# Attention scores as row-tiled products over one pool of PSUM banks, with keys kept on chip by head

## The chip, the cores and the metric

The kernel runs on one core of a Trainium2 chip. The metric is the device time of one execution in microseconds. Inputs and outputs are in DRAM; the host only lays the arrays out (transposed and padded copies) before the launch.

The engines are TensorE (PE in the profile, with its weight loads as PEld), VectorE (DVE), ScalarE (ACT), GpSimd (POOL) and SyncE (SP, which only issues transfers here). TensorE writes its products into PSUM, eight banks of 128 partitions by 512 floats.

## The reference, cut to what matters

```python
x = A_x                                            # [1, 2048, 448]
g = sigmoid((x * gate_w).sum(-1, keepdims=True))
# a: attention, 16 heads of 28
q, k, v = split_heads(x @ wqkv)
p = softmax(einsum("bhqd,bhkd->bhqk", q, k) * 28 ** -0.5)
a = merge_heads(einsum("bhqk,bhkd->bhqd", p, v)) @ wo
# b: layer norm and MLP, 448 -> 1792 -> 448
h = gelu(einsum("bsd,df->bsf", layernorm(x), w1) + b1)
b = einsum("bsf,fd->bsd", h, w2) + b2
return g * a + (1 - g) * b
```

All of it is float32. The kernel's fast matrix products take a rounded form of float32 (`F32R`, rows marked fp32r). Where more precision is needed an operand is split into a rounded part "hi" and the rest "lo", and hi x hi, hi x lo and lo x hi are added up (in the scores before also lo x lo).

## The kernel before, in words

The work has three stages, one after the other on TensorE, whose order is that of the text (`manual_schedule` for PE at the launch). The other engines' order is chosen by the framework's scheduler.

*Projections (L123 to L243).* The 2048 tokens are four chunks of 512 (`NC`, `CH`). For each chunk seven products of 128 columns give q and k for all heads, written to DRAM as hi and lo (`qk`, L164), and four products give v, padded to 32 columns a head with a column of ones (`vs`). Layer-norm statistics run beside them.

*MLP (L355 to L422).* For each chunk and each of 14 blocks of the hidden layer, `mlp1` accumulates 11 products into one bank (`ph`), ScalarE computes GELU twice (rounded and full), POOL takes the difference, and `mlp2` adds 12 products into four banks (`acc2`). The sum goes to DRAM (`gbs`).

*Attention (L503 to L567).* Heads are taken four at a time (`NG` = 4 groups), queries 512 at a time: 16 chunks (g, c). For each of 16 blocks of 128 keys (k), a step does this:

- `scores` (L522), twice for two heads each: one product a head. Its stationary operand has 113 rows: k hi, lo, hi, lo stacked, 28 rows each, and a row of ones; its moving operand has q hi, lo, lo, hi stacked in the same way and a row with the negative maximum of each query's scores. So one product gives all four hi/lo terms less the maximum. The two heads go to a pair of banks (`psc`, two pairs in turn).
- one exponential on ScalarE for each pair, 128 x 1024 (L531).
- `pv_mm` (L534) for the step before: four products of 32 columns, one for each head, side by side in one bank (`ppv`), in full float32 (two weight halves each, so eight rows in the profile).
- `filler.run` (L314): row maxima, below.

At a chunk's end `finish` (L459) copies the values' bank (L464), sends the four rows of sums through DRAM so that their reciprocals (L467) come back spread over all partitions (L465, L469, L471), normalises on POOL (L475 to L477), and in four later steps projects with `wo` (`project`, L449), adding into `acc` (L455). `STEPS` says in which steps k these pieces come. `finish_last` does the same for the last chunk without the trip through DRAM.

*Row maxima.* `row_max` (L245) finds the maximum of the scores from the hi parts alone: for each chunk 64 products of 28 rows (a head's 128 queries against 512 keys, L280), each in the row group of its head (`32 * j`), each with a `reduce_max` on VectorE (L282), then a transpose and a write to DRAM (`ms`); 65 turns a chunk, 1040 in all. `Filler` spreads these turns evenly over the products of the MLP (400 of them, `MLP_MAX`) and the steps of attention (the other 640), three at a time. Their banks are three of their own (`mp3` in the MLP, `paux` in attention; `paux` also serves `project`). Their keys and queries (`kd`, `qd`) are loaded separately.

*Loads for attention.* `load_k` fills `kring`, twelve buffers that were the MLP's w1 tiles, with one head's half of the keys, hi and lo, twice over; `load_q` fills `qring`. The first group's come late in the MLP (L411 to L416); values (`load_v`), `wo` and the MLP's sums (`acc`, L515, with bias and gate on POOL at L517 and L518) come at the start of attention.

Of the kernel before, what the change touches and what calls it, by code (L numbers as in the profile page):

```python
# [15 lines left out]
P = 128  # L16
S = 2048
# [13 lines left out]
MLP_MAX = 400  # L31
# [7 lines left out]
def kernel(ctx: ExitStack, tc: tile.TileContext, xt, wqk, wv, wo, xk, w1, b1, w2, b2,  # L39
# [22 lines left out]
    ones = dram.tile([8, P], F32, name="ones")  # L62
    rls = dram.tile([NG * NC, 4, CH], F32, name="rls")

    one_t = const.tile([8, P], F32, name="one_t")
# [6 lines left out]
    aq = ctx.enter_context(tc.tile_pool(name="aq", bufs=1, side="right"))  # L72

# [6 lines left out]
    kring = []  # L80
    qring = [aq.tile([P, 4, CH], F32R, name=f"qst{i}") for i in range(3)]

    def load_w(f, pool1, pool, stage):
        r1 = stage.tile([P, 4, P], F32, name="r1")
        nc.sync.dma_start(r1, w1[f])
        t = pool1.tile([P, 8, P], F32R, name=f"w1f{f}")
        w1h[f], w1l[f] = t[:, 0:4], t[:, 4:8]
        if f >= 2:
            kring.append(t.rearrange("p a b -> p (a b)"))
# [11 lines left out]
    def ln_load(c, t):  # L101
# [4 lines left out]
        lnx[c, t] = my.tile([P, CH], F32, name="xr", bufs=4)  # L106
        nc.sync.dma_start(lnx[c, t], xt[t, :, cs])

    def ln_apply(c, t):
        if t == 0:  # L110
            yh[c] = qring[c % 2]
            yl[c] = my.tile([P, 3, CH], F32R, name="yl")
# [10 lines left out]
    with tc.tile_pool(name="qx", bufs=2) as qx, tc.tile_pool(name="qo", bufs=3) as qo, \  # L123
            tc.tile_pool(name="qw", bufs=1) as qw, tc.tile_pool(name="qp", bufs=8, space=PSUM) as qp:
        wh, wl = {}, {}

# [26 lines left out]
        def qk_tile(c, m):  # L153
            ps = qp.tile([P, CH], F32, name="ps")
# [12 lines left out]
        def v_tile(tt):  # L167
            c, i = divmod(tt, TPC)
            sl = slice(i * P, (i + 1) * P)
            ps = qp.tile([P, CH], F32, name="ps")  # L170
# [28 lines left out]
        def ln_turn():  # L199
            ps = qp.tile([P, CH], F32, name="ps")  # L200
# [44 lines left out]
    def row_max(pool):  # L245

        kds, qds = {}, {}

        def load(n):
            g, c = divmod(n, NC)  # L250
            if c == 0:
                kds[g] = mpool.tile([P, S], F32R, name="kd")
                for j in range(4):
                    r = D + (4 * g + j) * DH
                    pool[1].dma_start(kds[g][32 * j:32 * j + DH].bitcast(F32), qk[0, r:r + DH])
            qds[n] = mpool.tile([P, CH], F32R, name="qd")
            for j in range(4):
                r = (4 * g + j) * DH
                pool[1].dma_start(qds[n][32 * j:32 * j + DH].bitcast(F32), qk[0, r:r + DH, c * CH:(c + 1) * CH])

        def close(n, mf):
            g, c = divmod(n, NC)
            ps = pool[0]()
# [3 lines left out]
            pool[1].dma_start(ms[g][:, c * CH:(c + 1) * CH].rearrange("j (i x) -> j i x", x=P), mt.bitcast(F32))  # L267
# [3 lines left out]
        for n in range(NG * NC):  # L271
            kd, qd = kds[n // NC], qds[n]
            mx = mpool.tile([P, 4, TPC, 4], F32, name="mx")
            done = 0
            for i in range(TPC):
                for k in range(4):
                    for j in range(4):
                        ps = pool[0]()
# [16 lines left out]
    class Filler:  # L295


        def __init__(self):
            self.pool = [None, None]
            self.it = row_max(self.pool)  # L300
# [3 lines left out]
        def spread(self, pool, queue, upto, slots):  # L304
            self.pool[:] = pool, queue
            self.first, self.upto, self.slots, self.slot = self.done, upto, slots, 0

        def run(self, n=1, group=1):
# [4 lines left out]
            group = min(group, self.upto - self.done)  # L313
            if due >= group:  # L314
                for _ in range(group):
                    next(self.it, None)
                    self.done += 1
# [3 lines left out]
    HS = S // 2  # L321
    NK = 12
    kst, qst = {}, {}
    nk = nq = 0

    def load_k(g, j, h):

        nonlocal nk
        t = kring[nk % NK]
        if nk < NK:  # L330
            nc.sync.dma_start(t[4 * DH:4 * DH + 1].bitcast(F32),
                              ones.rearrange("a b -> (a b)").rearrange("(o t) -> o t", o=1))
        nk += 1
        kst[g, j, h] = t
        r0 = D + (4 * g + j) * DH
        src = qk[:, r0:r0 + DH, h * HS:(h + 1) * HS]
        for r in range(0, 4 * DH, 2 * DH):
            nc.sync.dma_start(t[r:r + 2 * DH].bitcast(F32), src)

    def load_q(g, c):  # L340

        nonlocal nq
        t = qring[(0, 2, 1)[nq % 3]]
        nq += 1
        qst[g, c] = t
        cs = slice(c * CH, (c + 1) * CH)
        for i, n in enumerate((0, 1, 1, 0)):
            nc.sync.dma_start(t[i * DH:(i + 1) * DH].bitcast(F32),
                              qk[n, 4 * g * DH:4 * (g + 1) * DH, cs].rearrange("(j p) t -> p j t", p=DH))
        nc.sync.dma_start(t[4 * DH:4 * DH + 1].bitcast(F32), ms[g][:, cs].rearrange("(o j) t -> o j t", o=1))  # L350


    ak = ctx.enter_context(tc.tile_pool(name="ak", bufs=1, reuse_waits="tile"))
    with tc.tile_pool(name="mw", bufs=1, reuse_waits="tile") as mw, \
            tc.tile_pool(name="mh", bufs=3, reuse_waits="tile") as mh, \  # L355
            tc.tile_pool(name="mp1", bufs=1, space=PSUM, reuse_waits="tile") as mp1, \
            tc.tile_pool(name="mp3", bufs=3, space=PSUM, reuse_waits="tile") as mp3, \
            tc.tile_pool(name="mp2", bufs=4, space=PSUM, reuse_waits="tile") as mp2:
        hh, hl = {}, {}

        def mlp1(c, f):
            ps = mp1.tile([P, CH], F32, name="ph")
# [4 lines left out]
            for i, (a, b) in enumerate(ops):  # L367
                nc.tensor.matmul(ps, a, b, start=(i == 0), stop=(i == len(ops) - 1))  # L368
                filler.run(1, MG)
# [7 lines left out]
        acc2 = {}  # L377

        def mlp2(c, f):
            for i in range(TPC):  # L380
                if f == 0:
                    acc2[c, i] = mp2.tile([P, D], F32, name="acc2")
                sl = slice(i * P, (i + 1) * P)
                a = acc2[c, i]
                nc.tensor.matmul(a, hh[c, f][:, sl], w2h[f], start=(f == 0), stop=False)  # L385
                nc.tensor.matmul(a, hh[c, f][:, sl], w2l[f], start=False, stop=False)  # L386
                filler.run(2, MG)
                nc.tensor.matmul(a, hl[c, f][:, sl], w2h[f], start=False, stop=(f == NF - 1))  # L388
                filler.run(1, MG)
                if f == NF - 1:  # L390
# [6 lines left out]
                    (nc.sync if c < NC - 1 else nc.gpsimd).dma_start(gbs[tt], gb)  # L397

        prev = None
        for s in range(NC * NF):  # L400
            c, f = divmod(s, NF)
            if c == 0 and f + 2 < NF:
                load_w(f + 2, ak, mw, my)
            if s == FS:
                filler.spread(lambda: mp3.tile([P, 512], F32, name="pm"), nc.sync, MLP_MAX, (NC * NF - FS) * 23)
# [4 lines left out]
            if c == NC - 1 and f == 10:  # L410
                for j in range(4):  # L411
                    load_k(0, j, 0)
                load_q(0, 0)
                for j in range(4):
                    load_k(0, j, 1)
# [8 lines left out]
    def sb(name, bufs):  # L424
        return ctx.enter_context(tc.tile_pool(name=name, bufs=bufs, reuse_waits="tile"))

    av = sb("av", 2)
# [3 lines left out]
    psc = ctx.enter_context(tc.tile_pool(name="psc", bufs=2, space=PSUM, reuse_waits="tile"))  # L431
    ppv = ctx.enter_context(tc.tile_pool(name="ppv", bufs=1, space=PSUM, reuse_waits="tile"))
    paux = ctx.enter_context(tc.tile_pool(name="paux", bufs=3, space=PSUM, reuse_waits="tile"))

    vg = {}

    def load_v(g):
        vg[g] = av.tile([P, NT, P], F32, name="vg")
        for t in (slice(0, 4), slice(4, NT)):
            nc.scalar.dma_start(vg[g][:, t], vs[t, :, g, :].rearrange("t p d -> p t d"))  # L440

    def aux():
        return paux.tile([P, 512], F32, name="aux")

    woh = aw.tile([P, NG, D], F32R, name="woh")
    wol = aw.tile([P, NG, D], F32R, name="wol")
    acc = aw.tile([P, NT, D], F32, name="acc")

    def project(g, tt, oh, ol):  # L449

        po = aux()[:, :D]
# [32 lines left out]
    def finish_last(g, c, pv):  # L484
# [5 lines left out]
        psl = psc.tile([P, 2, CH], F32, name="sc")[:, 0]  # L490
# [12 lines left out]
    load_v(0)  # L503
    for g in range(NG):
        worw = ao.tile([P, D], F32, name="ob")
        nc.gpsimd.dma_start(worw, wo[:, g])
        nc.vector.tensor_copy(woh[:, g], worw)
        nc.gpsimd.tensor_sub(wol[:, g], worw, woh[:, g].bitcast(F32))

# [4 lines left out]
    for c in range(NC):  # L514
        nc.gpsimd.dma_start(acc[:, c * TPC:(c + 1) * TPC], gbs[c * TPC:(c + 1) * TPC].rearrange("t p d -> p t d"))  # L515
        for tt in range(c * TPC, (c + 1) * TPC):
            nc.gpsimd.tensor_add(acc[:, tt], acc[:, tt], b2b)  # L517
            nc.gpsimd.tensor_scalar(acc[:, tt], acc[:, tt], ngate[:, tt:tt + 1], None, op0=OP.mult)  # L518

    filler.spread(aux, nc.gpsimd, NG * NC * 65, (NG * NC - 2) * NT + LQ - 1)  # L520

    def scores(g, c, k, jj):  # L522

        h, kk = divmod(k, NT // 2)
        ps = psc.tile([P, 2, CH], F32, name="sc")
        for i in range(2):
            j = 2 * jj + i
            nc.tensor.matmul(ps[:, i], kst[g, j, h][:4 * DH + 1, kk * P:(kk + 1) * P],  # L528
                             qst[g, c][:4 * DH + 1, j], start=True, stop=True)
        t = ap.tile([P, 2, CH], F32, name="pt")  # L530
        nc.scalar.activation(t, ps, AF.Exp, scale=SCALE)  # L531
        return t

    def pv_mm(g, c, k, pv, pt):  # L534
        for j in range(4):
            nc.tensor.matmul(pv[32 * j:32 * j + 32, :], vg[g][:, k, 32 * j:32 * j + 32], pt[j // 2][:, j % 2],  # L536
                             start=(k == 0), stop=(k == NT - 1), skip_group_check=True)

    fin = None
    todo = []  # L540
    for g in range(NG):
        for c in range(NC):
# [78 lines left out]
```

## Time and profile before

| what | value |
|---|---|
| median of three runs | 1275.13 us (1271.72 to 1276.21) |
| profiled execution, its own time | 1273.18 us |
| its span in the profile | 1271.2 us |
| mean granted TensorE clock | 0.962 of full speed |
| instructions in the span | 16167 |
| bytes moved by DMA | 101.44 MB |
| MLP's last product on TensorE starts | 502.70 us |
| attention's last values products end | 1256.86 us |

The span runs from the first to the last instruction of the program; the time has 2.0 us around it. In the rows that follow, a group of instructions has its line, engine, operation, what it writes and reads with the shapes, its count, busy time, the mean length of one, and the idle time of its engine just before it with what ended that. A row of the timeline has start, length, engine, line and the number of instructions merged into it. A window's row gives the busy time of each engine in that stretch. Products overlap on TensorE, so a busy TensorE need not be at its peak.

### The profile page before, as it was taken

The numbers are of one execution on the slowest core, as the hardware profiler recorded it, in microseconds if no ns is written. First come the engines' busy times: TensorE is split into PE (matmuls) and PEld (weight loads), VectorE is DVE, ScalarE is ACT, GpSimd is POOL, SyncE is SP. The second block draws the span as 40 slices with busy tenths as digits, with TensorE's granted clock in tenths as the row PEclk, the third lists the DMA queues.
The fourth block names the chain that finished last, engine by engine and source line by source line (L and its number), as shares of the span: only waits on it lengthen the run. The fifth ranks groups of instructions, "written<-read, shape, count | busy, mean of one in ns | idle before, by whom it ended". The sixth has DMA issues, their size and how long they took to land.

```text
span 1271.2 us, 16167 instructions
## 1 busy us (share of the span) xinstructions
PE 1196.9 (94%) x6085; PEld 653.2 (51%) x6085; DVE 775.9 (61%) x1298; ACT 645.0 (51%) x765; POOL 322.5 (25%) x362
## 2 busy tenths in 40 slices
PE   7998999999999998196999999999999999999997
PEld 6886667766677665032444434444434444444433
DVE  3543377877776776144676757666756777676703
ACT  5243522212212211164677757767657767767784
POOL 4022952311222112356222121112022202211220
PEclk9999899999999999588999989999989999999998
DMA  8987740100101212532013142102412111210001
GB/s 281 295 279 261 203 108 25 46 9 1 37 16 47 72 53 82 147 112 59 17 40 75 53 103 78 38 10 56 99 64 61 44 31 38 76 35 34 25 24 58
DMA packets 56053, 101.44 MB, mean 80 GB/s; under 512 B 7352, under 2 KB 24240, under 8 KB 55528
## 3 DMA queue, kind: packets, MB, share of 16 engines
q1 hardware_dynamic: 41640, 82.53, 21.0%
q0 software_dynamic: 6016, 13.70, 4.0%
q10 hardware_dynamic: 8320, 4.19, 1.5%
q8 instruction: 48, 0.79, 0.3%
q14 instruction: 29, 0.24, 0.1%
HBM read 73.76 MB, written 26.49 MB: 79 GB/s over the span
## 4 chain that ended last, share of the span: by engine, by line
PE 75%; DMA 14%; POOL 5%; issue 2%; DVE 2%; ACT 1%; SPq 1%; ACTq 0%; POOLq 0%; DVEq 0%
PE sc L528 20%; PE pv L536 17%; PE ph L368 11%; PE aux L280 7%; PE pm L280 5%; PE acc L388 4%; PE acc L385 4%; PE acc L386 3%; DMA w1f<-qk 3%; DMA lt<-ob 2%; DMA xraw<-in_xt 2%; DMA acc<-gbs 2%; POOL acc L518 1%; PE ps L160 1%; PE aux L454 1%
## 5 line engine op out<-in xcount | busy, mean ns | idle before, releaser
L531 ACT ACTIVATE pt<-sc 128x1024 f32<-128x1024 f32 x512 | 496.5, 1021 | 230.6 <-PE sc L528 219.8
L282 DVE TENSOR_REDUCE mx<-aux 128x1 f32<-128x512 f32 x630 | 396.2, 683 | 176.8 <-PE aux L280 176.3
L528 PE MATMUL sc<-qst,w1f 113*128 113x512 f32 x1024 | 317.5, 429 | 33.9 <-ACT pt L531 33.9
L282 DVE TENSOR_REDUCE mx<-pm 128x1 f32<-128x512 f32 x394 | 248.1, 684 | 92.0 <-PE pm L280 91.6
L536 PE MATMUL pv<-pt,vg 128*32 128x512 f32 x2048 | 279.3, 617 | 0.0
L528 PEld LDWEIGHTS sc<-qst,w1f 113*128 113x128 f32 x1024 | 172.7, 191 | 152.5 <-ACT pt L531 83.6
L373 ACT ACTIVATE hh<-ph,b1s 128x512 fp32r<-128x512 f32 x56 | 38.4, 686 | 247.5 <-PE ph L368 247.5
L368 PE MATMUL ph<-qst,w1f 128*128 128x512 f32 x448 | 152.2, 413 | 7.1 <-ACT h L374 7.0
L280 PEld LDWEIGHTS aux<-kd,qd 28*128 28x128 f32 x630 | 45.0, 184 | 199.6 <-DVE mx L282 123.6
L375 POOL TENSOR_TENSOR hl<-h,hh 128x512 fp32r<-128x512 f32 x56 | 73.1, 1305 | 245.6 <-ACT h L374 244.3
L280 PE MATMUL aux<-kd,qd 28*128 28x512 f32 x630 | 116.7, 503 | 14.5 <-DVE mx L282 14.3
L368 PEld LDWEIGHTS ph<-qst,w1f 128*128 128x128 f32 x448 | 84.3, 192 | 34.3 <-issue 11.0
L536 PEld LDWEIGHTS pv<-pt,vg 128*32 128x32 f32 x2048 | 40.8, 108 | 92.5 <-issue 86.1
L388 PE MATMUL acc<-w2h,hl 128*128 128x448 f32 x224 | 87.2, 389 | 0.0
L385 PE MATMUL acc<-w2h,hh 128*128 128x448 f32 x224 | 84.5, 377 | 0.0
L386 PE MATMUL acc<-w2l,hh 128*128 128x448 f32 x224 | 82.0, 366 | 0.0
L465 POOL DMA_DIRECT2D lt<-ob x15 | 10.7, 716 | 254.3 <-DVE ob L464 254.3
L280 PE MATMUL pm<-kd,qd 28*128 28x512 f32 x394 | 73.5, 497 | 1.2 <-DVE mx L282 0.4
L368 PE MATMUL ph<-yl,w1f 128*128 128x512 f32 x168 | 69.5, 414 | 0.0
L455 DVE SCALAR_TENSOR_TENSOR acc<-aux,gate,acc 128x448 f32<-128x448 f32 x64 | 43.4, 678 | 39.3 <-PE aux L454 39.3
L280 PEld LDWEIGHTS pm<-kd,qd 28*128 28x128 f32 x394 | 28.2, 182 | 48.8 <-DVE mx L282 36.0
L160 PE MATMUL ps<-xh,wh 128*128 128x512 f32 x112 | 45.5, 406 | 7.0 <-ACT xh L147 6.4
(99 smaller groups left out, 980.8 us busy)
## 6 DMA issues: line engine op xcount, KB each, us to landing
qk<-hl SPq DMA_DIRECT2D x28, 512.0 KB
qst<-qk SPq DMA_DIRECT2D x64, 224.0 KB
w1f<-qk SPq DMA_DIRECT2D x64, 224.0 KB
xraw<-in_xt SPq DMA_DIRECT2D x16, 256.0 KB
vs<-vt SPq DMA_DIRECT2D x16, 256.0 KB
xr<-in_xt SPq DMA_DIRECT2D x16, 256.0 KB
rc<-rls POOLq DMA_DIRECT2D x60, 64.0 KB, 2.3
bxr<-in_xk SPq DMA_DIRECT2D x8, 448.0 KB
```

The source lines that it names most:

```text
L160: nc.tensor.matmul(ps, a, b, start=(i == 0), stop=(i == len(ops) - 1))
L280: nc.tensor.matmul(ps, qd[r, i * P:(i + 1) * P], kd[r, k * 512:(k + 1) * 512], start=True, stop=True)
L282: nc.vector.reduce_max(mx[:, j, i, k:k + 1], ps, axis=AX)
L368: nc.tensor.matmul(ps, a, b, start=(i == 0), stop=(i == len(ops) - 1))
L375: nc.gpsimd.tensor_sub(hl[c, f], h, hh[c, f].bitcast(F32))
L385: nc.tensor.matmul(a, hh[c, f][:, sl], w2h[f], start=(f == 0), stop=False)
L386: nc.tensor.matmul(a, hh[c, f][:, sl], w2l[f], start=False, stop=False)
L388: nc.tensor.matmul(a, hl[c, f][:, sl], w2h[f], start=False, stop=(f == NF - 1))
L455: nc.vector.scalar_tensor_tensor(acc[:, tt], po, gate[:, tt:tt + 1], acc[:, tt], op0=OP.mult, op1=OP.add)
L528: nc.tensor.matmul(ps[:, i], kst[g, j, h][:4 * DH + 1, kk * P:(kk + 1) * P], qst[g, c][:4 * DH + 1, j], start=True, stop=True)
L531: nc.scalar.activation(t, ps, AF.Exp, scale=SCALE)
L536: nc.tensor.matmul(pv[32 * j:32 * j + 32, :], vg[g][:, k, 32 * j:32 * j + 32], pt[j // 2][:, j % 2], start=(k == 0), stop=(k == NT - 1), s ...
```

## The change

Scores no longer use a stacked operand. The four heads of a group lie 32 partitions apart, so that each has a row group of TensorE to itself. Each head takes three products (lo x lo is left out), k hi x q hi (with the row of ones and the maximum, 29 rows), k lo x q hi and k hi x q lo (28 rows), added in one bank. The twelve products of a step are issued in an order and into banks that a class `Banks` works out while the program is built: it keeps an estimate, in units of one product, of when each of seven banks is free, and gives scores, row maxima and projections the banks that are free first. The eighth bank holds the values. The program has one PSUM tile of eight banks from start to end.

Keys are loaded once for each group, hi and lo apart (`khi`, `klo`), and `khi` serves the row maxima too, so `kd` goes. `load_khi`, `load_klo`, `load_q`, `load_qm` (the maxima) and `load_v` for the first group stand within the MLP; loads of later groups, `wo` and `acc` stand at given steps of attention, all on SP. Row maxima: 460 turns in the MLP, two or three at a time in attention, none in step k = 0. In attention all engines keep the order of the text. The step's order is now scores, row maxima, values of the step before, pieces of `finish`.

```diff
-MLP_MAX = 400
+MLP_MAX = 460
...
+    khi = [aq.tile([P, S], F32R, name=f"khi{g}") for g in range(2)]
+    qbuf = [(aq.tile([P, CH], F32R, name="qh0"), aq.tile([P, CH], F32R, name="ql0"))]
+    klob, vgb = [aq.tile([P, S], F32R, name="klo0")], [aq.tile([P, NT, P], F32, name="vg0")]
...
+    bank = ctx.enter_context(tc.tile_pool(name="pbank", bufs=1, space=PSUM)).tile([P, 8, CH], F32, name="bank")
...
-        r2 = stage.tile([P, D], F32, name="r2")
+        r2 = stage.tile([P, D], F32, name="r2", bufs=1)
...
-            kd, qd = kds[n // NC], qds[n]
+            kd, qd = khi[n // NC], qds[n]
...
-                        ps = pool[0]()
+                        ps = env.bank(j)
...
+            n = min(most, left, max(least, int(due)))
+            for _ in range(n):
+                next(self.it, None)
+                self.done += 1
+            return n
...
+    def load_khi(g):
+        for j in range(4):
+            r = D + (4 * g + j) * DH
+            nc.sync.dma_start(khi[g][32 * j:32 * j + DH].bitcast(F32), qk[0, r:r + DH])
+        nc.sync.dma_start(khi[g][DH:P:32].bitcast(F32),
+                          ones.rearrange("(a b) x -> a (b x)", a=1).partition_broadcast(4).rearrange("a o x -> a (o x)"))
...
+    def load_q(n):
+        g, c = divmod(n, NC)
+        qs[n] = qbuf[n % 3]
+        for i in range(2):
+            for j in range(4):
+                r = (4 * g + j) * DH
+                nc.sync.dma_start(qs[n][i][32 * j:32 * j + DH].bitcast(F32), qk[i, r:r + DH, c * CH:(c + 1) * CH])
+    def load_qm(n):
+        g, c = divmod(n, NC)
+        nc.sync.dma_start(qs[n][0][DH:P:32].bitcast(F32), ms[g][:, c * CH:(c + 1) * CH])
...
+            if s == FS - 1:
+                load_khi(0)
...
-            if c == NC - 1 and f == 10:
-                for j in range(4):
-                    load_k(0, j, 0)
-                load_q(0, 0)
-                for j in range(4):
-                    load_k(0, j, 1)
+            if c == 1 and f == 8:
+                load_khi(1)
+            if c == 2 and f == 10:
+                load_klo(0)
+                load_q(0)
+                load_qm(0)
+            if c == 3 and f == 1:
+                load_v(0)
...
+    class Banks:
...
+        def tile(self, tiled):
+            if tiled != self.tiled:
+                self.pe = max([self.pe + 0.4] if tiled else [r + 0.9 for r in self.rows])
+                self.rows = [self.pe] * 4
+                self.tiled = tiled
+        def product(self, j, ready):
+            self.pe = max(self.pe, self.rows[j], ready)
+            self.rows[j] = self.pe + 1
+            return self.pe + 1
+        def heads(self):
+            self.tile(True)
+            o = sorted(range(7), key=lambda b: self.free[b])[:4]
+            o = sorted(o[:2]) + sorted(o[2:])
+            ready = [max(self.pe, self.free[b]) for b in o]
+            turns = sorted((ready[j] + i, j, i) for j in range(4) for i in range(3))
+            end = [0.0] * 4
+            for _, j, i in turns:
+                end[j] = self.product(j, ready[j])
+            for i in (0, 2):
+                self.act = max(self.act, max(end[i:i + 2]) + 0.9) + 4.5
+                for b in o[i:i + 2]:
+                    self.free[b] = self.act + 0.5
+            return o, [t[1:] for t in turns]
+        def take(self, j=None):
+            b = min(range(7), key=lambda b: self.free[b])
+            self.tile(j is not None)
+            if j is None:
+                self.pe = end = max(self.pe, self.free[b]) + 2.8
+            else:
+                end = self.product(j, self.free[b])
+            self.dve = max(self.dve, end + 0.9) + 3
+            self.free[b] = self.dve + 0.5
+            return bank[:, b]
+        def values(self):
+            self.tile(False)
+            self.pe = max(self.pe, self.last) + 4.4
+            self.last = self.act + 0.5
...
+    def scores(g, c, k):
+        o, turns = banks.heads()
+        ks = slice(k * P, (k + 1) * P)
+        qh, ql = qs[g * NC + c]
+        for j, i in turns:
+            a, b, n = ((khi[g], qh, DH + 1), (klo[g], qh, DH), (khi[g], ql, DH))[i]
+            r = slice(32 * j, 32 * j + n)
+            nc.tensor.matmul(bank[:, o[j]], a[r, ks], b[r], start=(i == 0), stop=(i == 2))
+        pt = []
+        for i in (0, 2):
+            t = ap.tile([P, 2, CH], F32, name="pt")
+            nc.scalar.activation(t, bank[:, o[i]:o[i + 1] + 1:o[i + 1] - o[i]], AF.Exp, scale=SCALE)
+            pt.append(t)
+        return pt
...
+    with tc.manual_schedule(engines={E.SP, E.Pool, E.Activation, E.DVE}):
...
+                if g == 0:
+                    if k == 6:
+                        load_acc(c)
+                    if k == 14:
+                        gate_acc(c)
+                if k == 1 and n + 1 < NG * NC:
+                    load_q(n + 1)
+                if k == LQ and n + 1 < NG * NC:
+                    load_qm(n + 1)
+                if g + 1 < NG:
+                    if c == 1 and k == 4:
+                        load_klo(g + 1)
+                    if c == 2 and k == 4:
                         load_v(g + 1)
...
+                pt = scores(g, c, k)
+                if k:
+                    filler.run(1, 2, 3)
+                else:
+                    filler.run(1, 99, 0)
+                if todo:
+                    pv_mm(*todo)
+                    if todo[2] == NT - 1:
+                        fin = finish(todo[0], todo[1], todo[3])
+                        next(fin)
+                todo = (g, c, k, pv, pt)
                 if fin is not None and k in STEPS:
                     next(fin, None)
```

More of the change, by code (lines that the diff above doesn't have):

```diff
@@ L153, in qk_tile @@
         def qk_tile(c, m):
-            ps = qp.tile([P, CH], F32, name="ps")
+            ps = next_ps()
             ops = []
@@ L311, in run @@
+        def run(self, n=1, least=1, most=1):
             self.slot += n
             due = self.first + (self.upto - self.first) * min(1, self.slot / self.slots) - self.done
[L313 to L317, printed above, removed]
-    filler = Filler()
[L321 to L353, printed above, removed]
+            left = self.upto - self.done
@@ L447 @@
+    banks = Banks()
     acc = aw.tile([P, NT, D], F32, name="acc")
+    for i in (1, 2):
+        qbuf.append((aw.tile([P, CH], F32R, name=f"qh{i}"), aw.tile([P, CH], F32R, name=f"ql{i}")))
     def project(g, tt, oh, ol):
-        po = aux()[:, :D]
+        po = banks.take()[:, :D]
         nc.tensor.matmul(po, oh, woh[:, g], start=True, stop=False)
@@ L489, in finish_last @@
         ol = ao.tile([P, CH], F32R, name="ol")
-        psl = psc.tile([P, 2, CH], F32, name="sc")[:, 0]
+        psl = banks.take()
         tiles = [slice(i * P, (i + 1) * P) for i in range(TPC)]
@@ L513 @@
     nc.vector.tensor_scalar(ngate, gate, -1.0, 1.0, op0=OP.mult, op1=OP.add)
[L514 to L532, printed above, removed]
+    filler.spread(banks.take, nc.gpsimd, NG * NC * 65, (NG * NC - 2) * NT + LQ - 1)
+    def scores(g, c, k):
[12 more added lines that the diff above has]
+        return pt
     def pv_mm(g, c, k, pv, pt):
```

173 lines of the change are left out of this document (90 added, 83 removed).

## The prediction

> **What bounds the kernel now.** The page's engine rows first, then its chain of waits.
>
> ```profile
> PE 1196.9 (94%) x6085; PEld 653.2 (51%) x6085; DVE 775.9 (61%) x1298; ACT 645.0 (51%) x765; POOL 322.5 (25%) x362
> PE 75%; DMA 14%; POOL 5%; issue 2%; DVE 2%; ACT 1%; SPq 1%; ACTq 0%; POOLq 0%; DVEq 0%
> L280 PEld LDWEIGHTS aux<-kd,qd 28*128 28x128 f32 x630 | 45.0, 184 | 199.6 <-DVE mx L282 123.6
> ```
>
> TensorE is busy 94% of the span and holds 75% of the chain, but that is an average over three stages. So next the windows, one for each stage: first the projections, then the MLP, the change-over into attention, and attention.
>
> ```profile
> 0.00:200.00 200.00, 184.29 (x782) 144.23 (x782) 94.44 (x174) 77.25 (x133) 79.89 (x72) 0.97 0.72 227
> 200.00:520.00 320.00, 304.03 (x1396) 212.14 (x1395) 224.47 (x365) 67.88 (x110) 71.87 (x64) 0.98 0.13 43
> 520.00:575.00 55.00, 37.06 (x181) 14.04 (x181) 21.55 (x39) 26.64 (x29) 30.93 (x28) 0.75 0.46 120
> 600.00:1271.00 671.00, 654.72 (x3629) 276.29 (x3629) 424.34 (x703) 459.74 (x480) 123.16 (x186) 0.97 0.18 50
> ```
>
> The columns are length, busy PE, PEld, DVE, ACT and POOL, clock, DMA share and GB/s. Attention from 600 us on has PE busy 654.7 of 671 us while ACT has 459.7: PE sets the pace there. The stretch 520 to 575 does not run at that pace at all. Two timelines say why: one step of steady attention, and the change-over.
>
> ```profile
> 573.68 0.50 PE L280 MATMUL aux<-kd,qd 28*128 28x512 f32 x3
> 574.12 0.77 PEld L528 LDWEIGHTS sc<-qst,w1f 113*128 113x128 f32 x4 [0.25 <-issue]
> 574.12 1.20 PE L528 MATMUL sc<-qst,w1f 113*128 113x512 f32 x4
> 574.21 1.89 DVE L282 TENSOR_REDUCE mx<-aux 128x1 f32<-128x512 f32 x3 [0.67 <-PE aux L280]
> 574.95 1.94 ACT L531 ACTIVATE pt<-sc 128x1024 f32<-128x1024 f32 x2 [0.62 <-PE sc L528]
> 575.25 1.06 PE L536 MATMUL pv<-pt,vg 128*32 128x512 f32 x8
> 576.24 0.50 PE L280 MATMUL aux<-kd,qd 28*128 28x512 f32 x3
> ...
> 574.45 0.40 PE L528 MATMUL sc<-qst,w1f 113*128 113x512 f32 x1
> ...
> 574.69 0.39 PE L528 MATMUL sc<-qst,w1f 113*128 113x512 f32 x1
> ...
> 574.92 0.40 PE L528 MATMUL sc<-qst,w1f 113*128 113x512 f32 x1
> ```
>
> One step (four heads, 128 keys, 512 queries) goes from 573.68 to 576.24, **2.56 us**. PE spends 0.44 on three row-maximum products (573.68 to 574.12), 1.13 on four scores and 0.99 on the values. Three 28-row products stand in one row of 0.50 us, against 0.40 for one score product: different row groups run side by side. Scores follow each other every 0.234 us (574.45, 574.69, 574.92); the first takes 0.33, so 0.10 of it is a weight load with nothing in front. I split the lone 0.44 in the same way: 0.10 load, 0.234 stream, 0.10 until the array has left the row-tiled form.
>
> ```profile
> 502.70 0.37 PE L388 MATMUL acc<-w2h,hl 128*128 128x448 f32 x1
> 507.65 33.24 DMA w1f<-qk
> 542.40 2.14 PE L528 MATMUL sc<-qst,w1f 113*128 113x512 f32 x4 [8.26 <-ACT pt L531]
> ```
>
> The second bound: the MLP ends at about 503 us, and attention then waits for its stacked keys (33.24 us of the chain is that load), and its second step starts at 542.40. The pace of whole chunks is read from the copies of the values' bank.
>
> ```profile
> L464 DVE COPY ob<-pv x15: 690/691/692, 584.1 to 1219.8; 128x512 f32<-128x512 f32 x15
> ...
> 642.02 0.69 DVE L464 COPY ob<-pv 128x512 f32<-128x512 f32 x1 [0.28 <-PE pv L536]
> ```
>
> Chunk 0 ends at 584.1, chunk 1 57.9 us later at 642.0. From there to 1219.8 are 13 chunks, 44.4 us each. Sixteen steps of 2.56 and four projections of 0.61 (below) make 43.4: so 1.0 a chunk, 14 us in all, are stalls.
>
> **The change, part by part.**
>
> *Scores.* Four 113-row products (two halves of q, two of k, and the maximum stacked) become twelve of 28 or 29 rows, three in each of four row groups. Nothing in the trace shows a row group three or four deep. If its products follow at 0.234 like the 113-row ones, scores alone take 0.10 + 3 x 0.234 + 0.10 = 0.90 us. Row-maximum products now share that form and land on top of one group or another: depth four, 1.14. With the values' 0.99, a PE step is 1.89 without and **2.13** with row maxima, against 2.56.
>
> The cost that this hangs on is the weight load inside a row group. Its duration is 184 ns by the L280 row above. Hidden, it costs nothing; wholly exposed, each product after the first in its group costs 0.184 more. I take it as hidden: in the score rows four loads end within 0.77 us while the four products that use all those rows stream every 0.234, so a load runs beside the product before it on the same rows. The other end goes to the rivals. The Trainium skill's "TensorE: Matmul & The Clock Gate", Part 3, says that weight loads overlap matmuls in flight only when the row group differs. By that rule the third rival's sum holds; the 113-row loads here disagree with it, though no row here shows the row-tiled case.
>
> *Banks.* Before, four banks served scores and three the rest; now seven serve both. A hand count, from a phase's start at 0: the third products start at 0.57, the first exponential 0.50 later (574.45 to 574.95) at 1.07.
>
> ```profile
> 567.47 1.94 ACT L531 ACTIVATE pt<-sc 128x1024 f32<-128x1024 f32 x2 [0.61 <-PE sc L528]
> 568.39 1.02 ACT L531 ACTIVATE pt<-sc 128x1024 f32<-128x1024 f32 x1
> ```
>
> Exponentials start 0.92 apart and last 1.02, so ACT's floor is 1.84 a step: no bound yet. With 0.05 for release, the first pair of banks returns at 2.14, the second at 3.06. Row maxima start at 0.80, their reductions at 1.23; three take 1.89 with 0.69 for the last, so 0.60 apart: banks back at 1.96, 2.56, 3.16. The next phase wants four banks at 2.13 and has them at 1.96, 2.14, 2.14 and 2.56; its own three row maxima get theirs at 3.06, 3.06 and 3.16. So a step with three ends its phase near 3.57 instead of 3.27: 0.30 late, **2.43**. With two, the seventh bank lies idle and only the last row maximum is late, by under 0.1: I take 2.20. The bounds are 2.13 (the bank order avoids all waits) and 2.83 (the pairs of heads never overlap: 0.10 + 7 x 0.234 + 0.10 + 0.99).
>
> Of 1040 row-maximum turns 460 now fall in the MLP; 580 remain for 235 steps, of which 15 (k = 0) take none: 2.64 each, so 64% threes. The mean filled step is 0.64 x 2.43 + 0.36 x 2.20 = 2.35.
>
> *Output projection.* Four steps of a chunk carry one, with a bank from the same seven.
>
> ```profile
> 802.64 1.89 DVE L282 TENSOR_REDUCE mx<-aux 128x1 f32<-128x512 f32 x3 [0.71 <-PE aux L280]
> 805.80 1.89 DVE L282 TENSOR_REDUCE mx<-aux 128x1 f32<-128x512 f32 x3 [0.68 <-PE aux L280]
> ```
>
> Such a step lasts 3.16 instead of 2.56 here: 0.61, unchanged.
>
> *Sum of attention.* A full chunk is 15 x 2.35 + 1.89 + 4 x 0.61 = 39.6. Chunk 0 has no projection (37.1), thirteen are full (514.8), chunk 14 has row maxima in ten steps (23.5 + 6 x 1.89 + 2.4 = 37.2), chunk 15 none (32.7). Nine transposes of maxima remain here:
>
> ```profile
> L264 PE MATMUL aux<-ident,mf 128*16 128x128 f32 x10 | 2.8, 277 | 0.0
> ```
>
> At 0.28 each they are 2.5. Together **624 us**.
>
> *Change-over.* Keys, queries, maxima and values of group 0 load during the MLP, where DMA is 0.13 busy: that covers them. On SP they stand among the layer norm's loads and the MLP's writes, with the weight loads long over. The 39 us up to 542.4 go, but for what the steps below count; what is late next is one table load on ACT, which the last MLP products cover; I give it 1.
>
> *MLP.* Sixty more row-maximum products, twenty groups of three.
>
> ```profile
> 299.88 0.40 PE L368 MATMUL ph<-yl,w1f 128*128 128x512 f32 x1
> ...
> 300.21 0.51 PE L280 MATMUL pm<-kd,qd 28*128 28x512 f32 x3
> 300.65 0.73 PE L368 MATMUL ph<-qst,w1f 128*128 128x512 f32 x2
> ```
>
> From 299.88 to the second product of the last row (0.73 less its own 0.39, so 300.99) pass 1.11 us, of which two pitches are 0.47: 0.64 a group, 12.8 in all, on the path because PE is busy 304 of 320. One staging buffer for w2 instead of two can slow the weights of the first chunk; the cover is the 6 us of products that each weight block feeds. I take 0 and keep 10 us for the upper end.
>
> *Text order on the four other engines.* Behind the reciprocal of a chunk's sums (L467), DVE queues all row-maximum reductions, and PE their banks. Before, it waited like this:
>
> ```profile
> DVE lt L467 <- DMA lt<-ob: 35.0, 8, 13.6
> DMA to landing us min/median/max: 1.7/3.2/8.3
> ...
> qst<-qk SPq DMA_DIRECT2D x64, 224.0 KB
> ```
>
> Now it stands three steps, 7 us, behind the copy; the copy takes 0.69 and the transfer lands 3.2 after its issue in the median, so most are covered, though not one of 8.3. The loads beside them halve: queries were 64 pieces of 224 KB, and each half of q and k now moves once where it moved twice. On POOL the gating of acc stands ahead of the next chunk's DMA in group 0, but only POOL's own order holds it back, and POOL was busy 123 of 671 us in attention: nothing, or a few of the 6 us. The single bank tile leaves the first two stages their eight banks, and the loads moved to SP stand there in front of queries wanted a chunk later: nothing either. I keep the 14 us of stalls found above and add 6 for the first chunk.
>
> *End.* The last values product ends at 1254.11 + 2.75 = 1256.86; the span's end is 14.3 later; the tail is not changed.
>
> ```profile
> 1254.11 2.75 PE L536 MATMUL pv<-pt,vg 128*32 128x512 f32 x16
> ```
>
> **Sum.** Attention starts at 502.7 + 12.8 + 1 = 516.5; + 624 + 14.3 + 20 gives a span of 1175. The profiled execution took 1273.18 for its span of 1271.2, 2.0 around it, and lies 0.15% under the median of the three (1275.13). With 2.0 the time is 1177; I say **1176**.
>
> **The rivals.**
>
> *Banks bind harder.* For: what is free comes from two engines, and PE takes products in the order of an estimate; one late head holds all behind it. Against: the hand count meets only one late bank. If a filled step costs 2.60, half way to 2.83, 220 x 0.25 gives +55: 1231.
>
> *Text order stalls.* For: four engines lose the freedom to go past a waiting instruction. Against: the finish steps stand one step later than before. At 3.5 us a chunk beyond those counted, 15 x 3.5 = +53: 1229.
>
> *Weight loads are exposed in their row group (slower).* Place: the second to fourth product of each group. Price 0.184: 220 x 3 x 0.184 + 36 x 2 x 0.184 = +135, so 1311. It decides from 99 / 732 = 0.135 us exposed per product. For: no row shows a group deeper than one. Against: the hidden loads of the 113-row products. Products of different groups not running side by side at all is the same rival, much dearer, and speaks against the row of three in 0.50 us.
>
> **How the numbers follow.** My forecast, 1130 to 1215, has 0.66; the first two rivals together 0.19 (up to 1262); about no change 0.03, by parts of several; the third rival 0.12. The low end is every filled step at 2.13: 220 x 0.22 = 48 less, 1128. For the high end, 1262, the first rival's 1231 with 31 us of stalls and weight loads on top. 0.5% of this kernel is 6 us, about what a measurement can tell from no change. Faster 0.85, same 0.03, slower 0.12.
>
> **What would show it.** Twelve score products of a step in about 0.9 to 1.2 us, row starts 0.234 apart within a group: scores right; 0.40 apart: third rival. Score phases whose last head starts half a microsecond late, released by DVE or ACT: banks. Attention's first step at 515 to 520 with no DMA wait: change-over. Chunk copies 39 to 40 us apart: the step sum. Reductions stopped behind L467's successor: text order. ACT idle under 10% in attention would mean that ACT has become the bound and that my bank waits were too dear. Wrong altogether if a clock well under 0.97 is granted to sparse products.

## The result: 1846 us, slower by 45%, and the profile after

The changed kernel takes 1846.36 us (median of 4 runs, 1831.56 to 1858.25) against 1275.32: a ratio of **1.448** (95% interval 1.437 to 1.459). The profiled execution took 1847.08 for a span of 1845.3. The prediction, 1176 with a range up to 1262, had the sign wrong.

The page of the changed kernel: the engine rows, then the slices of PE and of the granted clock, each a fortieth of the span (46 us).

```profile
PE 1476.2 (80%) x8133; PEld 718.1 (39%) x8133; DVE 794.7 (43%) x1298; ACT 644.5 (35%) x765; POOL 308.8 (17%) x338
...
PE   8978999999997778777767777776777777767776
...
PEclk9998999999985686558878866765766656668698
```

In the first eleven slices, up to 507 us, PE is busy 70% or more and the clock is 0.8 or more. From the thirteenth slice on, in attention, PE's digits are 6 to 8 and the clock's 5 to 8, with a single 9. ACT and DVE have nearly the same work as before (644.5 us against 645.0, 794.7 against 775.9) and wait. The window of steady attention (length, busy PE, PEld, DVE, ACT, POOL, clock, DMA share, GB/s) and the waits in it:

```profile
600.00:1800.00 1200.00, 890.03 (x5459) 324.46 (x5459) 405.17 (x646) 457.80 (x473) 146.69 (x196) 0.69 0.07 18
```

```profile
ACT pt L608 <- PE bank L604: 735.0, 232, 7.8
POOL lt L535 <- DVE ob L534: 639.2, 15, 63.2
DVE mx L287 <- PE bank L285: 628.4, 276, 5.8
PEld bank L285 <- ACT pt L608: 393.8, 200, 3.1
PE bank L285 <- ACT pt L608: 281.0, 185, 2.4
```

ACT waits for scores, DVE for row-maximum products, and those products (L285) wait for ACT. Row maxima have no business with exponentials except through a bank. DMA is busy 0.07 of the time. A chunk takes 82.5 us: the fourteen between the first and the last copy of the values' bank in this row.

```profile
L534 DVE COPY ob<-bank x15: 691/692/692, 622.7 to 1777.9; 128x512 f32<-128x512 f32 x15
```

One good step and one bad step stand side by side in the timelines of PE and of ACT (start, length, engine, line, number merged, idle before).

```profile
897.93 0.50 PE L604 MATMUL bank<-qh,khi 29*128 29x512 f32 x4
898.26 0.40 PE L604 MATMUL bank<-qh,klo 28*128 28x512 f32 x4
898.50 0.40 PE L604 MATMUL bank<-ql,khi 28*128 28x512 f32 x4
898.74 0.40 PE L285 MATMUL bank<-khi,qd 28*128 28x512 f32 x3
899.07 1.06 PE L614 MATMUL bank<-pt,vg 128*32 128x512 f32 x8
900.08 0.50 PE L604 MATMUL bank<-qh,khi 29*128 29x512 f32 x2
901.00 0.49 PE L604 MATMUL bank<-qh,khi 29*128 29x512 f32 x1 [0.41 <-ACT pt L608]
...
903.12 0.50 PE L285 MATMUL bank<-khi,qd 28*128 28x512 f32 x1 [1.14 <-ACT pt L608]
904.03 0.58 PE L285 MATMUL bank<-khi,qd 28*128 28x512 f32 x1 [0.42 <-ACT pt L608]
904.55 1.94 PE L614 MATMUL bank<-pt,vg 128*32 128x512 f32 x8
```

```profile
899.01 1.94 ACT L608 ACTIVATE pt<-bank 128x1024 f32<-128x1024 f32 x2 [0.64 <-PE bank L604]
902.04 1.94 ACT L608 ACTIVATE pt<-bank 128x1024 f32<-128x1024 f32 x2 [1.10 <-PE bank L604]
```

The step from 897.93 to 900.08 takes 2.15 us, as the prediction's sum has it. In the next, the third head's product starts when the exponentials of the step *before* are through, and the two row maxima start when the first and the second exponential of their *own* step end (902.04 + 1.02 and 902.04 + 1.94). The eight values products behind these idle stretches (0.41, 1.14 and 0.42 us) take 1.94 us instead of 1.06. The windows of the good step and of these products (columns as above) have granted clocks of 1.00 and 0.50.

```profile
897.90:900.10 2.20, 2.20 (x29) 0.87 (x25) 1.17 (x3) 1.56 (x3) 0.00 (x0) 1.00 0.03 7
904.50:906.50 2.00, 2.00 (x10) 0.29 (x9) 0.69 (x1) 0.00 (x0) 0.00 (x0) 0.50 0.00 0
```

Why would a row maximum wait for an exponential of its own step? The plan gave it banks 1 and 3, which the exponential of the step before had been the last to read. The exponentials of its own step read banks 0 and 4, and 2 and 5. But in the built program, which lists the semaphore values that each instruction waits for, these two products wait for just those. The banks asked for lie *between* the two that are read. The third head is the same case: its bank 2 was last read by the first exponential of the step before, over banks 0 and 2, and it waits for the second, over banks 1 and 3.

A count over attention gives the same. Of 512 exponentials, 382 read two banks that are not neighbours. Of the waits on ACT for a bank that scores, row maxima and projections have, 62 name the last exponential that read this bank, and 268 name a later one that reads a bank on each side of it. So the theory: **the framework that sets the semaphores takes an exponential over banks 0 and 4 to hold everything from 0 to 4**, and so makes products wait for work that never touches their bank (the false-wait theory).

Two rivals: the plan for the pool truly collides on the chip (plan theory), or products of 28 rows let the clock drop whatever the waits (clock theory).

### The profile page after: what moved, and what is told of

The parts are those of the page before. It is cut to its first block, busy times and chain, and to the rows that moved or that the text cites. A ratio compares the mean times of both kernels' runs of the same rounds, so it can differ in the third digit from the quotient of the medians.

```text
span 1845.3 us, 20240 instructions
## 1 busy us (share of the span) xinstructions
PE 1476.2 (80%) x8133; PEld 718.1 (39%) x8133; DVE 794.7 (43%) x1298; ACT 644.5 (35%) x765; POOL 308.8 (17%) x338
## 5 line engine op out<-in xcount | busy, mean ns | idle before, releaser
L287 DVE TENSOR_REDUCE mx<-bank 128x1 f32<-128x512 f32 x1024 | 654.6, 686 | 740.3 <-PE bank L285 738.9
L608 ACT ACTIVATE pt<-bank 128x1024 f32<-128x1024 f32 x512 | 496.2, 1021 | 793.3 <-PE bank L604 783.9
L285 PE MATMUL bank<-khi,qd 28*128 28x512 f32 x1024 | 284.6, 564 | 302.3 <-ACT pt L608 295.0
L614 PE MATMUL bank<-pt,vg 128*32 128x512 f32 x2048 | 394.2, 851 | 0.0
L285 PEld LDWEIGHTS bank<-khi,qd 28*128 28x128 f32 x1024 | 116.7, 216 | 485.4 <-ACT pt L608 414.1
L604 PE MATMUL bank<-qh,khi 29*128 29x512 f32 x1024 | 185.0, 660 | 20.6 <-ACT pt L608 19.8
L388 PE MATMUL bank<-yh,w1f 128*128 128x512 f32 x448 | 153.9, 416 | 10.2 <-ACT h L394 8.9
L604 PE MATMUL bank<-qh,klo 28*128 28x512 f32 x1024 | 146.5, 523 | 0.0
L604 PE MATMUL bank<-ql,khi 28*128 28x512 f32 x1024 | 141.1, 504 | 0.0
L404 PE MATMUL bank<-w2h,hl 128*128 128x448 f32 x224 | 88.1, 393 | 0.0
```

The lines of the kernel that those rows point to most:

```text
L285: nc.tensor.matmul(ps, qd[r, i * P:(i + 1) * P], kd[r, k * 512:(k + 1) * 512], start=True, stop=True)
L287: nc.vector.reduce_max(mx[:, j, i, k:k + 1], ps, axis=AX)
L604: nc.tensor.matmul(bank[:, o[j]], a[r, ks], b[r], start=(i == 0), stop=(i == 2))
L608: nc.scalar.activation(t, bank[:, o[i]:o[i + 1] + 1:o[i + 1] - o[i]], AF.Exp, scale=SCALE)
```

## The experiments

### Neighbouring pairs, and one bank at a time

```diff
-            o = sorted(range(7), key=lambda b: self.free[b])[:4]
-            o = sorted(o[:2]) + sorted(o[2:])
+            late = lambda b: max(self.free[b:b + 2])
+            u = min(range(6), key=late)
+            w = min((b for b in range(6) if abs(b - u) > 1), key=late)
+            o = [u, u + 1, w, w + 1]
```

> Pairs of banks for an exponential are always neighbours (one contiguous 128x1024 read), otherwise as in the changed kernel. False-wait theory (an exponential over two banks that are not neighbours is taken to hold the banks between them too): nearly all of the loss goes, 1150 to 1260 us, granted clock back above 0.93. Plan theory (one pool of seven banks with an order worked out in advance truly collides): still above 1700 us. Clock theory (products of 28 rows do not keep TensorE's clock up, whatever the waits): still above 1600 us, clock below 0.82.

Measured for neighbouring pairs: 1230.6 us, ratio 0.967 (0.965 to 0.969) to the kernel before, clock 0.98.

```diff
-            nc.scalar.activation(t, bank[:, o[i]:o[i + 1] + 1:o[i + 1] - o[i]], AF.Exp, scale=SCALE)
+            for h in (0, 1):
+                nc.scalar.activation(t[:, h], bank[:, o[i + h]], AF.Exp, scale=SCALE)
```

> Banks and order of the changed kernel, but each exponential reads one bank, four a step instead of two. False-wait theory: the waits go, but ScalarE has four calls a step; with about 0.6 us a call (the 128x512 GELU took 0.688) that is 2.4 us a step: 1200 to 1330 us. Plan theory: no better than the changed kernel, 1800 us or more. Clock theory: clock below 0.82 and above 1600 us.

Measured: **1208.12 us, ratio 0.949** (0.947 to 0.951), clock 0.98. Its window in steady attention and its timelines of PE and ACT:

```profile
600.00:1180.00 580.00, 578.37 (x5325) 257.30 (x5321) 382.45 (x621) 475.83 (x925) 142.00 (x189) 1.00 0.12 34
```

```profile
801.76 0.51 PE L604 MATMUL bank<-qh,khi 29*128 29x512 f32 x4
802.10 0.41 PE L604 MATMUL bank<-qh,klo 28*128 28x512 f32 x4
802.34 0.40 PE L604 MATMUL bank<-ql,khi 28*128 28x512 f32 x4
802.57 0.61 PE L285 MATMUL bank<-khi,qd 28*128 28x512 f32 x3
803.11 1.06 PE L615 MATMUL bank<-pt,vg 128*32 128x512 f32 x8
804.11 0.73 PE L604 MATMUL bank<-qh,khi 29*128 29x512 f32 x4
```

```profile
800.57 2.07 ACT L609 ACTIVATE pt<-bank 128x512 f32<-128x512 f32 x4 [0.28 <-PE bank L604]
802.83 2.07 ACT L609 ACTIVATE pt<-bank 128x512 f32<-128x512 f32 x4 [0.19 <-PE bank L604]
```

The same banks, the same order of the same products, and twice as many exponentials: PE is busy 578 of 580 us at full clock, and a step with three row maxima takes 2.35. Both rivals fall here: the plan was kept, and so were the sparse products.

### Fixed banks, side by side and apart

```diff
-            o = sorted(range(7), key=lambda b: self.free[b])[:4]
-            o = sorted(o[:2]) + sorted(o[2:])
+            o = [0, 1, 2, 3]        # side by side;  [0, 2, 4, 6] apart
...
-            b = min(range(7), key=lambda b: self.free[b])
+            b = min((4, 5, 6), ...)  # side by side;  (1, 3, 5) apart
```

> No pool: scores always in banks 0 to 3 (pairs 0,1 and 2,3), row maxima and projections in 4 to 6. False-wait theory: no false waits; a head waits for the exponential of the step before, so 2.3 to 2.7 us a step, 1190 to 1300 us, clock above 0.93. Plan theory: also fast, as there is no pool. Clock theory: below 0.82 clock and above 1600 us.

> As the kernel with fixed banks, but with scores in banks 0, 2, 4, 6 (pairs 0,2 and 4,6) and the rest in 1, 3, 5, so that each exponential has a foreign bank between its two; the true conflicts are the same. False-wait theory: 1600 us or more, near the changed kernel. Plan and clock theories: the same time as with banks side by side, within 3%.

Measured: 1260.3 us (0.990, 0.987 to 0.992) side by side, and **1993.79** apart (one run). In both, with only three banks to give, the plan hands the third projection of the very last chunk the bank that still holds that chunk's sums, before the last quarter of them is read. So the output there is not the reference's; the work that is timed is the same. The windows, first side by side, then apart:

```profile
600.00:1230.00 630.00, 628.19 (x5333) 289.29 (x5326) 385.04 (x625) 448.29 (x463) 144.31 (x193) 1.00 0.12 31
```

```profile
600.00:1950.00 1350.00, 1010.41 (x5488) 364.38 (x5492) 409.60 (x651) 461.12 (x477) 146.20 (x196) 0.64 0.06 16
```

These two differ in nothing but bank numbers; the true conflicts are the same, one for one. A foreign bank between the two of an exponential costs 733 us. Apart, row maxima wait for exponentials in these two rows; side by side, no row of the waits has L285 waiting for ACT.

```profile
PEld bank L285 <- ACT pt L607: 482.7, 263, 2.8
PE bank L285 <- ACT pt L607: 327.4, 227, 2.1
```

The built programs say it directly: apart, 299 of 379 of PE's waits on an exponential for a bank name one that never read this bank; side by side, none of 510. This is the cleanest proof. It also gives a price for the pool: with pairs of neighbouring banks in both, fixed banks are 30 us slower than the pool (1260.3 against 1230.6).

### Does it matter that banks come free one at a time?

With 400 turns in the MLP (below), an exponential takes two banks where the plan gives neighbours (130 of them) and one bank otherwise (764).

```diff
-            for h in (0, 1):
-                nc.scalar.activation(t[:, h], bank[:, o[i + h]], AF.Exp, scale=SCALE)
+            if o[i + 1] == o[i] + 1:
+                nc.scalar.activation(t, bank[:, o[i]:o[i] + 2], AF.Exp, scale=SCALE)
+            else:
+                for h in (0, 1):
+                    nc.scalar.activation(t[:, h], bank[:, o[i + h]], AF.Exp, scale=SCALE)
```

> With 400 turns in the MLP, two banks in one exponential where the plan gives neighbours, one bank each where it doesn't: no exponential has a foreign bank between its two. False-wait theory: what matters is the bank between, not the number of exponentials, so it stays within 1.5% of 1195.5 us, though 512 to 1024 exponentials run. If the gain of one-bank exponentials came from banks that are freed one by one instead: slower by 20 us or more, towards the kernel with neighbouring pairs (1230.6).

Measured: 1196.12 us against 1195.5 with one bank throughout. It makes no difference in this mixture, in which a quarter of the 512 pairs (130) are read together; if pairs cost anything by themselves, most of that cost is left out here. Why pairs that are *forced* to be neighbours are 22 us slower than single banks (1230.6 against 1208.1) is not settled by it: the restricted choice and the later release both remain.

### The terms of the sum

```diff
-MLP_MAX = 460
+MLP_MAX = 400
```

> One-bank exponentials, and 400 row-maximum turns in the MLP instead of 460. The MLP's steps took 0.5 us longer each than before the change; if the sixty extra turns are the cause, the MLP ends 20 to 25 us earlier (last GELU near 505 instead of 528 us). Theory A (they cost the MLP more than they save in attention, because three banks and VectorE cannot take a group every 2.4 us): attention pays back about 12 us, total 1190 to 1204. Theory B (a turn costs the same in either place): the total stays within 5 us of 1208.

Measured: **1195.5 us, 0.937** (0.934 to 0.940). The last GELU, in rows with 460 and with 400 turns:

```profile
L393 ACT ACTIVATE hh<-bank,b1s x56: 669/688/691, 130.7 to 527.9; 128x512 fp32r<-128x512 f32 x56
```

```profile
L393 ACT ACTIVATE hh<-bank,b1s x56: 670/688/690, 133.0 to 508.8; 128x512 fp32r<-128x512 f32 x56
```

From the first GELU to the last are 397.2 and 375.8 us: 21.4 for twenty groups, 1.07 each. Attention pays back less: its chunks go from 40.4 to 41.2, 11 us in fourteen. Theory A's sum holds. Its reason is borne out too: in the traces of the MLP from 215 us on, groups follow each other every 2.61 us with 400 turns and every 2.43 with 460, and the third product of a group starts over 0.1 us behind the first in 5 of 103 groups and in 43 of 118.

```diff
-            o = sorted(o[:2]) + sorted(o[2:])
...
-            for i in (0, 2):
-                self.act = max(self.act, max(end[i:i + 2]) + 0.9) + 4.5
-                for b in o[i:i + 2]:
-                    self.free[b] = self.act + 0.5
+            for i in range(4):
+                self.act = max(self.act, end[i] + 0.9) + 2.4
+                self.free[o[i]] = self.act + 0.9
```

> One-bank exponentials, and the plan's estimate of ScalarE changed to match: four exponentials of 2.4 units, each of which frees its own bank, in the order in which the banks are free. If the waits that remain come from an estimate that still thinks in pairs, a chunk goes from 40.3 to 38 to 39.5 us, total 1180 to 1200. If they are true conflicts of seven banks: no change, 1203 to 1213.

Measured: 1209.69 us against 1208.12: no change. A better estimate in the plan brings nothing more.

```diff
-    with tc.manual_schedule(engines={E.SP, E.Pool, E.Activation, E.DVE}):
+    with ExitStack():
```

> One-bank exponentials, with the order of VectorE, ScalarE, GpSimd and SyncE in attention left to the scheduler as before the change. Text-order rival: the fixed order costs stalls of 1 to 3 us a chunk, so this is 15 us or more faster than 1208. My forecast's term (text order costs nothing to speak of): within 10 us of 1208, or slower, where the scheduler's estimate puts pieces of the finish ahead of row maxima.

Measured: 1227.7 us, 0.963 (0.960 to 0.966): slower by 20. The waits of the reciprocal for its DMA, first with the text's order (one-bank exponentials), then with the scheduler's:

```profile
DVE lt L537 <- DMA lt<-ob: 2.5, 1, 2.5
```

```profile
DVE lt L537 <- DMA lt<-ob: 21.6, 15, 5.6
```

In all, the reciprocal waits 19 us less in the text's order; that this is what the chunks gain is not shown. The place of the gain is: the copies of the values' bank follow every 40.4 us with the text's order and every 42.3 with the scheduler's, 27 us over fourteen chunks. At the very end it is the other way round. The last values products, with the text's order and with the scheduler's:

```profile
1181.37 3.32 PE L615 MATMUL bank<-pt,vg 128*32 128x512 f32 x16
1209.48 3.32 PE L615 MATMUL bank<-pt,vg 128*32 128x512 f32 x16
```

From their end to the span's end (1204.4 and 1226.6) are 19.7 us and 13.8; before the change it was 14.3. In the text's order the last addition of a tile stands ahead of the next tile's reciprocal on VectorE, so the four tiles of `finish_last` go one after the other.

```diff
-        r2 = stage.tile([P, D], F32, name="r2")
+        r2 = stage.tile([P, D], F32, name="r2", bufs=1)
```

> The kernel before with one staging buffer for w2 instead of two, nothing else. If this is what delays the changed kernel's MLP at its first blocks (5 to 9 us by the first six GELUs), it is 4 to 9 us slower than before, 1279 to 1284. If the delay comes from the other loads that the change puts in front: within 2 us of before.

Measured, in the kernel before: 1283.56 us, ratio 1.0066 (1.0045 to 1.0086): the single buffer alone costs about 8 us. The GELUs before the change and with the single buffer:

```profile
L373 ACT ACTIVATE hh<-ph,b1s x56: 671/688/691, 125.6 to 495.7; 128x512 fp32r<-128x512 f32 x56
L373 ACT ACTIVATE hh<-ph,b1s x56: 669/688/691, 128.7 to 505.2; 128x512 fp32r<-128x512 f32 x56
```

The last comes 9.5 us later. In the changed kernel with the same 400 turns it came at 508.8, so some 4 us of the MLP's delay have another cause, which stays open.

```diff
-                if k:
-                    filler.run(1, 2, 3)
-                else:
-                    filler.run(1, 99, 0)
+                filler.run(1, 2, 3)
```

> With 400 turns in the MLP and one-bank exponentials, row maxima also in a chunk's first step. The step sum says that fewer threes shorten the filled steps by about 0.1 us and lengthen the first ones by 0.3: no change within 5 us of 1195.5. If the copy of the values' bank then stands behind reductions and holds up the next values product: 10 us or more slower.

Measured: 1194.65 us, 0.937 (0.934 to 0.940): no change. All versions without a foreign bank inside an exponential are faster than the kernel before, the fixed banks side by side by only 1%.

## Why the prediction was wrong, step by step

*Banks* is the step that failed. It counted a bank as free when its last reader was done, and priced the worst case as pairs of heads that never overlap (2.83 us a step). The rival "banks bind harder" stopped at 2.60. The runs showed 82.5 us a chunk, about 5 us a step, through a mechanism that was in no rival: a step in the read of an exponential was taken for an interval, so that products waited for exponentials of other banks, some of their own step. The diff showed it, in the slice `o[i]:o[i + 1] + 1:o[i + 1] - o[i]`. For ACT's own time the stride costs nothing, as the sum has it (1021 ns on average before and after); what it does to the waits was never asked.

The size follows from one loss on top of another. In steady attention PE was idle 310 of 1200 us, 26%: of a chunk's 82.5 us that is 21, and 61 are busy, where the one-bank kernel needs 40 for the same products. So about half of the loss is waiting. The other half is longer busy time, and the granted clock of 0.69 accounts for nearly all of it (0.69 x 61 = 42). The clock is a consequence: with the waits gone, the same products ran at 1.00. So the prediction's last sign, a low clock "granted to sparse products", did appear, but it was not the sparseness that brought it.

*Scores* was right. Within a row group the three products start 0.33 and 0.24 us apart (897.93, 898.26, 898.50), four groups side by side; with three row maxima on top, the values start 1.14 us after the first score (899.07), the number in the sum. *Weight loads*, the third rival, fell: 0.24 apart leaves no room for an exposed load of 0.18. The loads of the third products stand beside the second products, in the same four row groups:

```profile
898.27 0.20 PEld L604 LDWEIGHTS bank<-ql,khi 28*128 28x128 f32 x4
```

The Trainium skill's "TensorE: Matmul & The Clock Gate", Part 3, says that weight loads overlap matmuls in flight only when the row group differs; the row-tiled loads here disagree with that sentence.

*The step and chunk sum* came out once the false waits are out: 40.4 us a chunk with one-bank exponentials and 41.9 with neighbouring pairs, where the prediction has 39.6 and 1.0 of stalls. The closer one is in part luck, for that kernel frees its banks one by one, which the hand count does not have. The filled step quoted above took 2.35 with three row maxima; the prediction gives such a step 2.43, and its 2.35 is the mean over steps with two and three.

*Change-over* was right in kind: in the changed kernel the first scores come 0.3 us behind the MLP's last product, with no load in between.

```profile
538.77 0.37 PE L404 MATMUL bank<-w2h,hl 128*128 128x448 f32 x1
539.07 0.51 PE L604 MATMUL bank<-qh,khi 29*128 29x512 f32 x4
```

It comes at 539 instead of 516.5 (at 535.0 with one-bank exponentials), mainly for two mis-sized terms. *MLP*: twenty groups of three cost 21.4 us, not 12.8, because with less time between groups the third product often comes late. *One staging buffer*, costed at nothing, costs 8 in the kernel before.

*Text order* was costed at nothing beyond the stalls of before; it saves about 20 us, 27 in the chunks less 6 at the end. In the chunks the second rival pointed the wrong way. *End* has the tail as not changed, and that is wrong: the same order lengthens it from 14.3 to 19.7 us.

So of the 670 us between forecast and result, 638 go with one-bank exponentials (1846.4 to 1208.1), 616 with neighbouring pairs. The profiled run with one-bank exponentials, 1206.14, lies 30 us above the forecast. By its trace some 18 of them come before the first scores, about 4 in chunk 0, 5 in the last chunk and 5 in the tail; the fourteen chunks between took 565 us, about what the sum gives them with its 14 us of stalls.

## What to carry to other kernels

When a change makes an operand's address or stride depend on data structures (here, on which banks happen to be free), look at the waits that it produces before counting engine time: a strided access may be booked as everything between its ends. Two accesses to one bank each can be far cheaper than one to two distant banks, even on an engine that then has twice the calls. And an idle time on TensorE that spreads over every step is to be priced with the clock that it costs, not only with its own length.

## What the runs showed of the hardware that was not expected

Two kernels whose PE is busy three quarters of the time were granted a clock of only 0.64 and 0.69 over a millisecond. In the changed kernel's window of 1200 us the trace has 230 idle stretches of PE, about one a step, with a median of 1.2 us and none over 2.4; with one-bank exponentials, PE busy over 99%, the same products ran at 1.00. Halving the exponential to one bank raises ACT's time for a step by 7% (four in 2.07 us against two in 1.94). Twelve products in four row groups, each with its own weight load, start in three waves 0.33 and 0.24 us apart, where four 113-row products one after another started every 0.234.
